# Delta rule and routed experts on one core: groups of 128 tokens, a state update from raw keys, two inverses interleaved

## The chip, the cores and the metric

One core of a Trainium2 chip runs the whole program as one launch. The metric is the device time in microseconds; the median of three runs of the kernel before is 737.12 us (735.65 to 737.18).

## The reference

```python
def _attn_ref(q, k, v, beta):          # q, k, v: (4, 8, 768, 48) f32; beta: (4, 8, 768)
    k_n = k / (np.linalg.norm(k, axis=-1, keepdims=True) + 1e-06)
    state = np.zeros((B, H, D, D)); y = np.zeros_like(q)
    for t in range(S):
        kt, vt, bt = k_n[:, :, t], v[:, :, t], beta[:, :, t, None]
        y[:, :, t] = np.einsum('bhd,bhde->bhe', q[:, :, t], state)
        v_old = np.einsum('bhde,bhd->bhe', state, kt)
        state = state + bt[:, :, :, None] * np.einsum('bhd,bhe->bhde', kt, vt - v_old)
    return y
def _moe_ref(x, token_ids, w1, w2):    # x: (3072, 384); w1: (8, 384, 1024); w2: (8, 1024, 384)
    expert_idx = token_ids * np.int64(2654435761) % np.int64(E)
    for e in range(E):
        mask = expert_idx == e
        out[mask] = np.maximum(x[mask] @ w1[e], 0.0) @ w2[e]
```

The answers of the delta rule, with the heads side by side, are the rows x of the expert stage.

## The kernel before

Phase 1 is the delta rule, phase 2 the experts; between them stands a scratch tensor in DRAM (x_scratch). All arithmetic is float32. Instructions go to each engine's queue in the order in which the program writes them (`tc.manual_schedule()`).

Phase 1 cuts the 768 tokens into 24 chunks of C = 32. On the 128 partitions lie the four batches times 32 tokens of a chunk, for 8 heads (four pairs u, each with two heads r). Four chunks make a group; there are six groups.

For each chunk `load_k` and `load_q` bring K and Q in four transfers each, `turn_k` turns them on TensorE (`psT`, evicted by ScalarE into KQ), and `gram` multiplies keys with keys and queries (`psG`, evicted into Gsb). `masks_of` makes the masked matrix MT from Gsb on GpSimd. This runs AHEAD = 10 chunks before the chain.

For each group `invert` makes, for 32 (chunk, head) pairs at a time, the inverse of a triangular matrix 32 by 32: the head takes the turn NTt, the sums of squares ssq, a Sqrt on ScalarE (root), some ten small VectorE instructions, and Ni and the diagonal of U on GpSimd; then for each of 31 columns j a product into tmp (L244) and a sum into U (L241), the rows cut into an upper and a lower half; the last instruction turns U into TU. The main loop takes the pieces of this generator after each chunk, by a fixed count.

The chain runs over the chunks c. `ask(c, 0)` multiplies the keys with the state (psX); R = V1 - psX on VectorE (L283); `solve` multiplies Tz with R (psW), and ScalarE evicts it as W (L298); `update` adds Kz times W to the state in psS (L309), which stays in PSUM, and four ScalarE copies bring it to SBUF (L318); `ask(c, 1)` and `answer` make psY, evicted as x_sb (L330) and written to x_scratch on SP's queue. Tz, Kz (keys spread over two halves with zeros) and V1 are made on GpSimd a chunk ahead.

`routing()` counts the tokens of each expert and computes the gather lists gidx and gx, with the products gp (L448); the loop takes one of its pieces per chunk from c = 4 on. At c = 16 the rest is taken and the first expert's weights are loaded. Phase 2 gathers 128 rows at a time and runs two matrix products per expert.

Of the kernel before, what the change touches and what calls it, by code (L numbers as in the profile page):

```python
# [18 lines left out]
def kernel(  # L19
# [59 lines left out]

    with ExitStack() as phase1:  # L80
# [7 lines left out]
        AHEAD = 10  # L88
        NK = AHEAD + 3
# [16 lines left out]

        K4s = [st.tile([P, HU, 2, DP], F32, name=f"K4_{i}") for i in range(NK)]
        Q4s = [st.tile([P, HU, 2, DP], F32, name=f"Q4_{i}") for i in range(3)]
        Ss = [st.tile([P, 2, H, 2, D], F32, name=f"S_{i}") for i in range(2)]
        psS = ps_s.tile([P, 2, BANK], F32, name="psS")  # L110
        tid32 = rt.tile([P, NTC, 2], I32)
        beta_i = st.tile([P, NG, C], F32)
        beta_h = rt.tile([C, S], F32)
        beta_t = rt.tile([C, NU, B, H], F32)
        beta_q = rt.tile([P, NG, GC, H], F32)
        iota_i = rt.tile([P, P], I32)
        iota_f = rt.tile([P, P], F32)
# [11 lines left out]
        def load_k(c, eng):  # L129
            dst = K4s[c % NK].rearrange("p u r d -> p (u r) d")  # L130
            for b in range(B):
                eng.dma_start(out=dst[quarter(b), :, 0:D], in_=k_r[b][c * C:(c + 1) * C])

        def load_q(c, eng):
            dst = Q4s[c % 3].rearrange("p u r d -> p (u r) d")
            for b in range(B):
                eng.dma_start(out=dst[quarter(b), :, 0:D], in_=q_r[b][c * C:(c + 1) * C])

        Vs, V1s, Kzs = {}, {}, {}

        def load_v(c):
            Vs[c] = wk.tile([P, H, D], F32, tag="V", bufs=4, name="V")
# [3 lines left out]
        def routing_setup():  # L146
            nc.vector.tensor_copy(iota_f, iota_i)

        KQs, MTs, Gsbs, TUs, Tzs, n_toks = {}, {}, {}, {}, {}, {}

        def turn_k(c, a, src):
            if a == 0:
                KQs[c] = wk.tile([P, HU, 2, P], F32, tag="KQ", bufs=AHEAD + 1, name="KQ")
            ps = ps_z.tile([P, HU, P], F32, tag="z", name="psT")
# [4 lines left out]
        def gram(c):  # L159
            g, cc = divmod(c, GC)  # L160
            if cc == 0:
                Gsbs[g] = wk.tile([P, GC, HU, 2, 2 * C], F32, tag="Gsb", bufs=2, name="Gsb")
            KQ = KQs[c]
            ps = [ps_z.tile([P, HU, 2 * C], F32, tag="z", name=f"psG{r}") for r in range(2)]
            for u in range(HU):
                for r in range(2):
                    for b in range(B):
                        nc.tensor.matmul(  # L168
                            ps[r][quarter(b), u, :], lhsT=KQ[half(r), u, 0, quarter(b)],
                            rhs=KQ[half(r), u, :, quarter(b)], start=(u == 0), stop=True,  # L170
                            skip_group_check=True, tile_position=(DP * r, C * b))
            for r in range(2):
                nc.scalar.activation(Gsbs[g][:, cc, :, r, :], ps[r], ACT.Copy)  # L173

        def masks_of(c):
            G = Gsbs[c // GC][:, c % GC].rearrange("p u r y -> p (u r) y")
            MTs[c] = wk.tile([P, H, 2, C], F32, tag="MT", bufs=AHEAD + 1, name="MT")
            nc.gpsimd.tensor_tensor(MTs[c], G[:, :, None, C:].to_broadcast([P, H, 2, C]),  # L178
                                    mask2[:, None].to_broadcast([P, H, 2, C]), op=ALU.mult)
# [14 lines left out]
        def spread_k(c):  # L194

            Kzs[c] = wk.tile([P, H, 2, D], F32, tag="Kz", bufs=2, name="Kz")
            nc.gpsimd.tensor_tensor(  # L197
                Kzs[c],
                K4s[c % NK].rearrange("p u r d -> p (u r) d")[:, :, None, 0:D].to_broadcast(
                    [P, H, 2, D]),  # L200
                kmask[:, None, :, None].to_broadcast([P, H, 2, D]), op=ALU.mult)

        def invert(g):

            G = Gsbs.pop(g).rearrange("p c u r y -> p (c u r) y")
            NTt = wk.tile([P, C, C], F32, tag="NTt", bufs=1, name="NTt")
            nc.vector.transpose(NTt, G[:, :, 0:C].rearrange("p x j -> p j x"))
            ssq = wk.tile([P, C], F32, tag="ssq", bufs=2, name="ssq")
            nc.vector.tensor_scalar(out=ssq, in0=NTt.rearrange("p j i -> p (j i)")[:, ::C + 1],
                                    scalar1=1e-30, scalar2=None, op0=ALU.max)  # L210
            root = wk.tile([P, C], F32, tag="root", bufs=2, name="root")
            nc.scalar.activation(root, ssq, ACT.Sqrt)
            yield
            rn = wk.tile([P, C], F32, tag="rn", bufs=2, name="rn")
            nc.vector.reciprocal(rn, root)
            nc.vector.tensor_tensor(rn, rn, ssq, op=ALU.mult)
            nc.vector.tensor_tensor(root, root, rn, op=ALU.add)
            nc.vector.tensor_scalar(out=root, in0=root, scalar1=0.5, scalar2=1e-6,
                                    op0=ALU.mult, op1=ALU.add)
            nc.vector.tensor_tensor(rn, root, root, op=ALU.mult)  # L220
            nc.vector.reciprocal(rn, rn)
            d = wk.tile([P, C], F32, tag="d", bufs=2, name="d")
            nc.vector.tensor_tensor(d, rn, beta_i[:, g], op=ALU.mult)
            nd = wk.tile([P, C], F32, tag="nd", bufs=2, name="nd")
            nc.vector.tensor_scalar(out=nd, in0=d, scalar1=-1.0, scalar2=None, op0=ALU.mult)
            Ni = wk.tile([P, C, C], F32, tag="Ni", bufs=1, name="Ni")
            U = wk.tile([P, C, C], F32, tag="U", bufs=1, name="U")
            nc.gpsimd.memset(U, 0.0)
            nc.gpsimd.tensor_tensor(Ni, NTt, nd[:, None, :].to_broadcast([P, C, C]), op=ALU.mult)
            nc.gpsimd.tensor_copy(U.rearrange("p c i -> p (c i)")[:, ::C + 1], d)  # L230
            n_toks[g] = wk.tile([P, NX], F32, tag="ntok", bufs=3, name="ntok")
            nc.vector.transpose(n_toks[g], root)
            yield
            def term(lo, hi, j, last):

                n, m = hi - lo, C - 1 - j
                if not last:
                    tmps[lo] = wk.tile([P, L * L], F32, tag=f"tmp{lo}", bufs=2, name="tmp")
                tmp = tmps[lo][:, 0:n * m].rearrange("p (n m) -> p n m", n=n)
                if last:  # L240
                    nc.vector.tensor_tensor(U[:, lo:hi, j + 1:], U[:, lo:hi, j + 1:], tmp,  # L241
                                            op=ALU.add)
                else:
                    nc.vector.tensor_tensor(tmp, U[:, lo:hi, j:j + 1].to_broadcast([P, n, m]),  # L244
                                            Ni[:, j:j + 1, j + 1:].to_broadcast([P, n, m]),
                                            op=ALU.mult)

            tmps = {}
            lower = iter([(j, last) for j in range(L, C - 1) for last in (False, True)])
            for j in range(C - 1):  # L250
                hi = min(j + 1, L)
                term(0, hi, j, False)
                nxt = next(lower, None)
                if nxt:
                    term(L, nxt[0] + 1, *nxt)
                term(0, hi, j, True)
                yield
            TUs[g] = wk.tile([P, NX, C], F32, tag="TU", bufs=2, name="TU")
            nc.vector.transpose(TUs[g].rearrange("p x i -> p i x"),  # L259
                                U.rearrange("p c i -> p i c"))  # L260
            yield
# [6 lines left out]
        def ask(c, a, ps):  # L268
            S0 = Ss[c % 2]
            for u, b in slots():  # L270
                nc.tensor.matmul(ps[quarter(b), u], lhsT=KQs[c][:, u, a, quarter(b)],
                                 rhs=S0[:, b // 2, 2 * u + b % 2].rearrange("p r d -> p (r d)"),
# [3 lines left out]
        def old_values(c):  # L276
# [5 lines left out]
            R = wk.tile([P, H, D], F32, tag="R", bufs=2, name="R")  # L282
# [5 lines left out]
        def solve(c, R):  # L288
# [8 lines left out]
            W = wk.tile([P, H, D], F32, tag="W", bufs=2, name="W")  # L297
# [3 lines left out]
        def update(c, W):  # L301
            Kz = Kzs.pop(c)
            S1 = Ss[(c + 1) % 2]
            for u in range(HU):
                for e in range(2):
                    for r in range(2):
                        for p in range(2):
                            rows = slice(DP * p, DP * p + DP)
                            nc.tensor.matmul(  # L309
# [174 lines left out]
        with tc.manual_schedule():  # L484
            for t in Q4s + K4s:
                nc.gpsimd.memset(t[:, :, :, D:], 0.0)
            for c in range(3):
                load_q(c, nc.gpsimd)
# [226 lines left out]
```

## Time and profile before

| | us |
|---|---|
| median of 3 runs | 737.12 |
| the profiled execution's own time | 736.42 |
| its span | 734.8 |
| TensorE busy in the span | 564.0 (77%) |
| VectorE busy | 304.5 (41%) |
| GpSimd busy | 232.5 (32%) |
| ScalarE busy | 140.3 (19%) |

The span runs from the first to the last instruction of the profiled execution; the rest of its own time lies around it. Busy time is the time in which an engine works on some instruction, and idle time is only worth something on the engine that others wait for. Shares are means over stages with different limits.

### The profile page before, as it was taken

Reading aid. Unit: us, or ns where it says so; the run is one execution under the profiler, and the core shown is the slowest. Engines: PE = TensorE matmul, PEld = TensorE weight load, DVE = VectorE, ACT = ScalarE, POOL = GpSimd, SP = SyncE. Lnnn points to the kernel's source line nnn. Section 1 sums busy time; section 2 is a strip of 40 time slices with the busy share of each in tenths; the row PEclk is TensorE's granted clock in tenths of the full one; section 3 lists DMA queues with packets and bytes.
Section 4 is the critical chain, followed back from the end, with each engine's and each line's share of the span. In section 5 each row is a group of like instructions: output and inputs, shape, how many; then the busy total and the mean of one; then the engine's idle time right before and its main releaser. Section 6 shows DMA issues by size and latency. Waiting matters only on the chain. (4 is left out here: it accounts for less than half of the span.)

```text
span 734.8 us, 16900 instructions
## 1 busy us (share of the span) xinstructions
PE 564.0 (77%) x7252; PEld 368.1 (50%) x7252; DVE 304.5 (41%) x805; ACT 140.3 (19%) x291; POOL 232.5 (32%) x256
## 2 busy tenths in 40 slices
PE   3660657468456564577729999999999999999996
PEld 2440546457455454566614555546455554645553
DVE  4269695895997677594021101111110111111100
ACT  2430324224224141133400000010000000000000
POOL 7783714445335233343342120303021130101101
PEclk9999968778777576768968999999999999999999
DMA  8621114233232011152159432214333010000000
GB/s 124 121 47 31 35 26 87 47 75 65 46 71 62 17 25 41 26 194 59 41 205 385 155 119 95 75 65 139 97 121 122 12 49 0 32 0 22 14 12 19
DMA packets 87115, 54.72 MB, mean 74 GB/s; under 512 B 69626, under 2 KB 80966, under 8 KB 87040
## 3 DMA queue, kind: packets, MB, share of 16 engines
q1 hardware_dynamic: 81536, 42.02, 21.5%
q0 software_dynamic: 5504, 11.61, 5.3%
q8 instruction: 58, 0.95, 0.6%
q14 instruction: 17, 0.14, 0.1%
HBM read 45.74 MB, written 11.01 MB: 77 GB/s over the span
## 5 line engine op out<-in xcount | busy, mean ns | idle before, releaser
L618 PE MATMUL o_ps<-w_sb,h_sb 128*128 128x384 f32 x512 | 169.9, 486 | 0.0
L607 PE MATMUL h_ps<-xT,w_sb 128*128 128x512 f32 x384 | 167.5, 596 | 0.0
L618 PEld LDWEIGHTS o_ps<-w_sb,h_sb 128*128 128x128 f32 x512 | 95.2, 190 | 61.1 <-issue 1.0
L607 PEld LDWEIGHTS h_ps<-xT,w_sb 128*128 128x128 f32 x384 | 73.5, 192 | 90.7 <-issue 88.8
L244 DVE TENSOR_TENSOR tmp<-U,Ni 128x48 f32<-128x48 f32 (+32 forms) x276 | 98.8, 385 | 42.6 <-POOL U L230 36.9
L591 POOL DMA_INDIRECT xg<-x_scratch,gx x32 | 32.7, 1022 | 168.7 <-PE xT_ps L600 148.8
L294 PE MATMUL psW<-R,Tz 64*64 64x48 f32 x736 | 35.4, 263 | 63.3 <-DVE R L283 63.3
L241 DVE TENSOR_TENSOR U<-U,tmp 128x48 f32<-128x48 f32 (+32 forms) x276 | 83.1, 326 | 0.2
L612 DVE TENSOR_SCALAR h_sb<-h_ps 128x512 f32<-128x512 f32 x32 | 22.1, 692 | 144.8 <-PE h_ps L607 144.8
L622 POOL DMA_INDIRECT out_dram<-o_sb,gidx x32 | 32.1, 1002 | 137.4 <-ACT o_sb L621 87.4
L178 POOL TENSOR_TENSOR MT<-Gsb,mask 128x512 f32<-128x512 f32 x24 | 31.6, 1316 | 127.5 <-ACT Gsb L173 125.8
L294 PEld LDWEIGHTS psW<-R,Tz 64*64 64x64 f32 x736 | 32.3, 178 | 67.9 <-DVE R L283 39.8
L610 ACT ACTIVATE h_sb<-h_ps 128x512 f32<-128x512 f32 x32 | 19.1, 597 | 183.8 <-PE h_ps L607 183.8
L318 ACT ACTIVATE S<-psS 48x384 f32<-48x384 f32 x92 | 44.6, 485 | 26.2 <-PE psS L309 24.6
L601 DVE COPY xT<-xT_ps 128x384 f32<-128x384 f32 x32 | 17.7, 553 | 73.8 <-PE xT_ps L600 72.5
L168 PE MATMUL psG<-KQ 48*32 48x64 f32 x1536 | 26.6, 288 | 24.1 <-ACT KQ L157 23.4
L621 DVE COPY o_sb<-o_ps 128x384 f32<-128x384 f32 x16 | 8.9, 558 | 84.6 <-PE o_ps L618 79.9
L157 ACT ACTIVATE KQ<-psT 128x512 f32<-128x512 f32 x48 | 28.5, 597 | 74.3 <-PE psT L156 74.2
L184 POOL TENSOR_TENSOR Tz<-TU,kmask 128x512 f32<-128x512 f32 x24 | 25.9, 1079 | 52.5 <-DVE TU L259 32.3
L197 POOL TENSOR_TENSOR Kz<-K,kmask 128x768 f32<-128x768 f32 x24 | 36.5, 1519 | 4.0 <-PE psS L309 4.0
L168 PEld LDWEIGHTS psG<-KQ 48*32 48x32 f32 x1536 | 21.2, 137 | 29.5 <-ACT KQ L157 27.4
L309 PE MATMUL psS<-W,Kz 64*48 64x48 f32 x1472 | 29.4, 248 | 7.4 <-ACT W L298 7.3
(123 smaller groups left out, 532.6 us busy)
## 6 DMA issues: line engine op xcount, KB each, us to landing
w_sb<-in_moe_w_dram SPq DMA_DIRECT2D x16, 1536.0 KB, 7.5
K<-in_k_dram SPq DMA_DIRECT2D x96, 48.0 KB, 2.7
V<-in_v_dram SPq DMA_DIRECT2D x96, 48.0 KB, 2.2
x_scratch<-x_sb SPq DMA_DIRECT2D x24, 192.0 KB, 2.6
Q<-in_q_dram SPq DMA_DIRECT2D x52, 48.0 KB, 2.3
Q<-in_q_dram POOLq DMA_DIRECT2D x44, 48.0 KB, 2.6
xg<-x_scratch,gx POOLq DMA_INDIRECT x32, 6.3
out_dram<-o_sb,gidx POOLq DMA_INDIRECT x32, 2.6
```

The lines of the kernel that those rows point to most:

```text
L168: nc.tensor.matmul(ps[r][quarter(b), u, :], lhsT=KQ[half(r), u, 0, quarter(b)], rhs=KQ[half(r), u, :, quarter(b)], start=(u == 0), stop=Tr ...
L178: nc.gpsimd.tensor_tensor(MTs[c], G[:, :, None, C:].to_broadcast([P, H, 2, C]), mask2[:, None].to_broadcast([P, H, 2, C]), op=ALU.mult)
L197: nc.gpsimd.tensor_tensor(Kzs[c], K4s[c % NK].rearrange("p u r d -> p (u r) d")[:, :, None, 0:D].to_broadcast([P, H, 2, D]), kmask[:, None ...
L241: nc.vector.tensor_tensor(U[:, lo:hi, j + 1:], U[:, lo:hi, j + 1:], tmp, op=ALU.add)
L244: nc.vector.tensor_tensor(tmp, U[:, lo:hi, j:j + 1].to_broadcast([P, n, m]), Ni[:, j:j + 1, j + 1:].to_broadcast([P, n, m]), op=ALU.mult)
L294: nc.tensor.matmul(psW[rows, h], lhsT=Tz[rows, h].rearrange("p e i -> p (e i)"), rhs=R[rows, h], start=(h == 0), stop=True, skip_group_che ...
L309: nc.tensor.matmul(psS[half(r), p, D * (2 * u + e):D * (2 * u + e) + D], lhsT=Kz[rows, 2 * u + r, e], rhs=W[rows, 2 * u + r], start=(c == ...
L318: nc.scalar.activation(S1[half(r), :, part, r], new[half(r), :, part], ACT.Copy)
L591: nc.gpsimd.indirect_dma_start(out=xg, out_offset=None, in_=x_dram[:, :], in_offset=bass.IndirectOffsetOnAxis(ap=idx, axis=0), bounds_chec ...
L607: nc.tensor.matmul(h_ps[:, :width], lhsT=w1_sb[:, co, fo * P:(fo + 1) * P], rhs=xT[:, co, :width], start=(co == 0), stop=(co == CO - 1))
L618: nc.tensor.matmul(o_ps, lhsT=h_sb[:, fo, col * P:(col + 1) * P], rhs=w2_sb[:, fo, :], start=(fo == 0), stop=(fo == FO - 1))
L622: scat = nc.gpsimd.indirect_dma_start(out=out[:, :], out_offset=bass.IndirectOffsetOnAxis(ap=idx, axis=0), in_=o_sb, in_offset=None, bound ...
```

## The change

K and Q are loaded for turning by 128 tokens of one batch (`load_turn`, one transfer where there were four) and turned by `turn`; KQ holds a whole group. Raw keys are loaded once more by chunk (`load_k`) as the update's left operand. `gram` evicts keys with keys and keys with queries apart, GK (already in the order that the turn NTt reads) and GQ. `spread_k` and Kz are gone: `update` takes 32 rows of raw keys of a batch for both heads of a pair, 128 columns, and psS has one bank for each batch. `invert` becomes `head`, `strand` and `tail`; `together` deals out one instruction of each strand in turn, and a group's second half runs with the next group's first half. `fill` spends a budget of 5500 by the diff's own cost numbers per chunk, and `fill_until` finishes what the next group needs. The prologue turns four groups and makes the grams of three and the whole of inverse 0 before the chain begins. Routing has four pieces in the prologue and two per chunk from c = 17; gp is cut into 8 parts of 3 products. The first weights are loaded after c = 20. The pools are smaller: z 2, x 1 (in place of 3 and 2), R and W one buffer each. Phase 2 is the same.

```diff
-        def load_k(c, eng):
-            dst = K4s[c % NK].rearrange("p u r d -> p (u r) d")
+        def load_turn(g, a, b, eng):
+            dst = (KTs, QTs)[a][b].rearrange("p u r d -> p (u r) d")
+            eng.dma_start(out=dst[:, :, 0:D], in_=(k_r, q_r)[a][b][g * NB:(g + 1) * NB])
+        def load_k(c):
+            dst = K4s[c % 3].rearrange("p u r d -> p (u r) d")
...
+        def turn(g, a, b, eng=nc.scalar):
+            src = (KTs, QTs)[a][b]
+            ps = ps_z.tile([P, HU, NB], F32, tag="z", name="psT")
             for u in range(HU):
                 nc.tensor.transpose(ps[:, u, :], src[:, u].rearrange("p r d -> p (r d)"), ident)
-            nc.scalar.activation(KQs[c][:, :, a, :], ps, ACT.Copy)
+            copy_out(eng, KQs[g][:, :, a, b, :], ps)
...
             for r in range(2):
-                nc.scalar.activation(Gsbs[g][:, cc, :, r, :], ps[r], ACT.Copy)
+                nc.scalar.activation(GKs[g][:, :, cc, :, r].rearrange("p j u -> p u j"),
+                                     ps[r][:, :, 0], ACT.Copy)
+                nc.scalar.activation(GQs[c][:, :, r], ps[r][:, :, 1], ACT.Copy)
...
+        def head(g, first):
+            nc.vector.transpose(NTt, GKs.pop(g).rearrange("p j c u r -> p j (c u r)"))
+            nc.gpsimd.memset(U, 0.0)
...
             nc.scalar.activation(root, ssq, ACT.Sqrt)
-            yield
+            yield 1600
...
+            (nc.vector if first else nc.gpsimd).tensor_tensor(
+                Ni, NTt, nd[:, None, :].to_broadcast([P, C, C]), op=ALU.mult)
...
+        def strand(g, c0, c1, j0, j1):
+            U, Ni = Us[g], Nis[g]
+            for j in range(max(j0, c0), j1):
+                n, m = min(j + 1, c1) - c0, C - 1 - j
...
+                nc.vector.tensor_tensor(t, U[:, c0:c0 + n, j:j + 1].to_broadcast([P, n, m]),
+                                        Ni[:, j:j + 1, j + 1:].to_broadcast([P, n, m]),
+                                        op=ALU.mult)
+                yield 75 + 1.04 * n * m
+                nc.vector.tensor_tensor(U[:, c0:c0 + n, j + 1:], U[:, c0:c0 + n, j + 1:], t,
+                                        op=ALU.add)
+                yield 75 + 1.04 * n * m
...
+                    yield from head(g, False)
+                both = []
+                if g > 1:
+                    both += [strand(g - 1, 0, L, L, C - 1), strand(g - 1, L, C, L, C - 1)]
+                if g == 1:
+                    both += [strand(g, 0, L // 2, 0, L), strand(g, L // 2, L, L // 2, L)]
+                elif g < NG:
+                    both += [strand(g, 0, L, 0, L)]
+                yield from together(*both)
...
         def update(c, W):
-            Kz = Kzs.pop(c)
...
-                            nc.tensor.matmul(
-                                psS[half(r), p, D * (2 * u + e):D * (2 * u + e) + D],
-                                lhsT=Kz[rows, 2 * u + r, e], rhs=W[rows, 2 * u + r],
-                                start=(c == 0 and u == 0 and e == 0), stop=True,
-                                skip_group_check=True, tile_position=(DP * p, DP * r))
+            S1, K4 = Ss[(c + 1) % 2], K4s[c % 3]
+            for u, b in slots():
+                nc.tensor.matmul(psS[:, b, 2 * D * u:2 * D * u + 2 * D],
+                                 lhsT=K4[quarter(b), u].rearrange("p r d -> p (r d)"),
+                                 rhs=W[quarter(b), 2 * u:2 * u + 2].rearrange("p r d -> p (r d)"),
+                                 start=(c == 0 and u == 0), stop=True, skip_group_check=True,
+                                 tile_position=(C * b, 0))
...
+        GRAM_AT = {0: 12, 1: 13, 2: 14, 3: 15, 5: 16, 6: 17, 7: 18, 8: 19,
+                   10: 20, 11: 21, 12: 22, 13: 23}
+        TURN_AT = {(3, 1): t4[0:2], (4, 0): t4[2:4], (4, 1): t4[4:8],
+                   (7, 1): t5[0:1], (8, 0): t5[1:3], (8, 1): t5[3:5], (9, 0): t5[5:6],
+                   (9, 1): t5[6:8]}
+        LOAD_AT = {0: t4[0:4], 1: t4[4:8], 5: t5[0:4], 6: t5[4:8]}
...
+            for c in range(GC):
+                gram(c)
+            steps(route, 4)
+            fill_until(0)
+            for g in range(1, GC):
...
+                for b in range(B):
+                    for a in range(2):
+                        turn(g, a, b)
+                if g < GC - 1:
+                    for c in range(GC * g, GC * g + GC):
+                        gram(c)
...
+            for c in range(NU):
...
+                W = solve(c, R)
+                for t in TURN_AT.get((c, 0), ()):
+                    turn(*t)
+                if c < NU - 1:
                     update(c, W)
+                answer(c, W, psY)
+                for t in TURN_AT.get((c, 1), ()):
+                    turn(*t)
+                if c in GRAM_AT:
+                    gram(GRAM_AT[c])
+                for t in LOAD_AT.get(c, ()):
+                    load_turn(*t, nc.sync)
+                if c + 1 < NU:
+                    scale_v(c + 1)
+                    if c + 1 == GC * (g + 1):
+                        fill_until(g + 1)
+                    spread_t(c + 1)
+                    masks_of(c + 1)
+                fill(5500)
+                if c >= 17:
+                    steps(route, 2)
```

## Rows read from the trace of the kernel before

**Rows 1.** Busy us of PE, PEld, DVE, ACT, POOL by stage; clock, DMA share, GB/s.

```profile
0.00:77.30 77.30, 33.48 (x724) 24.85 (x724) 43.37 (x130) 19.95 (x43) 49.88 (x87) 1.00 0.45 77
77.30:339.00 261.70, 160.97 (x4628) 141.65 (x4628) 207.63 (x582) 79.04 (x171) 104.71 (x94) 0.73 0.26 59
```

**Rows 2.** The chain that ended last, around the end of phase 1.

```profile
370.98 3.73 DMA x_scratch<-x_sb
```

**Rows 3.** Timeline of ACT, a late step: start, duration, what.

```profile
343.01 0.49 ACT L298 ACTIVATE W<-psW 128x384 f32<-128x384 f32 x1 [2.09 <-PE psW L294]
344.70 2.02 ACT L318 ACTIVATE S<-psS 48x384 f32<-48x384 f32 x4 [1.20 <-PE psS L309]
```

**Rows 4.** Timeline of PE, from 247 to 351 us.

```profile
247.13 2.77 PE L448 MATMUL gp<-hi,lo 128*128 128x52 f32 x12 [11.94 <-DVE lo L443]
...
334.06 1.95 PE L294 MATMUL psW<-R,Tz 64*64 64x48 f32 x32 [2.80 <-DVE R L283]
336.75 1.53 PE L309 MATMUL psS<-W,Kz 64*48 64x48 f32 x64 [0.74 <-ACT W L298]
...
343.65 0.93 PE L309 MATMUL psS<-W,Kz 64*48 64x48 f32 x63 [0.74 <-ACT W L298]
...
347.28 0.87 PE L271 MATMUL psY<-S,KQ 128*32 128x96 f32 x32
348.08 1.13 PE L294 MATMUL psW<-R,Tz 64*64 64x48 f32 x32
349.96 0.96 PE L309 MATMUL psS<-W,Kz 64*48 64x48 f32 x61 [0.74 <-ACT W L298]
```

**Rows 5.** Timeline of DVE, from 71 to 115 us.

```profile
71.12 1.92 DVE L207 STREAM_TRANSPOSE NTt<-Gsb 128x1024 f32<-128x1024 f32 x1
...
74.16 0.35 DVE L215 RECIPROCAL rn<-root 128x32 f32<-128x32 f32 x1 [0.30 <-ACT root L212]
...
81.73 2.38 DVE L244 TENSOR_TENSOR tmp<-U,Ni 128x31 f32<-128x31 f32 x2 [5.38 <-POOL U L230]
...
99.22 0.55 DVE L283 TENSOR_TENSOR R<-V,psX 128x384 f32<-128x384 f32 x1
99.68 0.42 DVE L244 TENSOR_TENSOR tmp<-U,Ni 128x256 f32<-128x256 f32 x1
100.02 0.55 DVE L241 TENSOR_TENSOR U<-U,tmp 128x64 f32<-128x64 f32 x2
100.60 0.54 DVE L244 TENSOR_TENSOR tmp<-U,Ni 128x240 f32<-128x240 f32 x2
...
114.06 2.17 DVE L259 STREAM_TRANSPOSE TU<-U 128x1024 f32<-128x1024 f32 x1
```

**Rows 6.** Busy time of each engine while one inverse runs, columns as before.

```profile
81.73:114.06 32.33, 18.29 (x654) 15.94 (x652) 31.30 (x95) 11.55 (x25) 12.29 (x11) 0.79 0.21 44
```

**Rows 7.** POOL's instructions by line: busy us, mean ns, idle before.

```profile
L197 POOL TENSOR_TENSOR Kz<-K,kmask 128x768 f32<-128x768 f32 x24 | 36.5, 1519 | 4.0 <-PE psS L309 4.0
...
L178 POOL TENSOR_TENSOR MT<-Gsb,mask 128x512 f32<-128x512 f32 x24 | 31.6, 1316 | 127.5 <-ACT Gsb L173 125.8 <-DVE beta_t L521 1.7
L184 POOL TENSOR_TENSOR Tz<-TU,kmask 128x512 f32<-128x512 f32 x24 | 25.9, 1079 | 52.5 <-DVE TU L259 32.3 <-PE psW L294 19.6 <-PE psT L156 0.6
...
L191 POOL TENSOR_TENSOR V<-V,ntok 128x384 f32<-128x384 f32 x24 | 21.4, 892 | 0.0
L229 POOL TENSOR_TENSOR Ni<-NTt,nd 128x1024 f32<-128x1024 f32 x6 | 14.1, 2353 | 5.5 <-DVE nd L225 5.5
```

**Rows 8.** Timeline of the prologue, from 14 to 19 us.

```profile
14.77 1.11 PE L156 MATMUL psT<-ident,K 128*128 128x128 f32 x4
...
15.67 1.06 PE L156 MATMUL psT<-ident,Q 128*128 128x128 f32 x4
...
17.42 1.18 PE L168 MATMUL psG<-KQ 48*32 48x64 f32 x64 [0.69 <-ACT KQ L157]
...
18.57 0.66 ACT L173 ACTIVATE Gsb<-psG 128x256 f32<-128x256 f32 x2 [1.21 <-PE psG L168]
```

More of the change, by code (lines that the diff above doesn't have):

```diff
@@ L155, in turn_k, with copy_out @@
+        def copy_out(eng, out, in_):
+            if eng is nc.scalar:
+                nc.scalar.activation(out, in_, ACT.Copy)
+            else:
+                nc.vector.tensor_copy(out, in_)
+        def turn(g, a, b, eng=nc.scalar):
+            if g not in KQs:
+                KQs[g] = wk.tile([P, HU, 2, B, NB], F32, tag="KQ", bufs=4, name="KQ")
+            src = (KTs, QTs)[a][b]
+            ps = ps_z.tile([P, HU, NB], F32, tag="z", name="psT")
             for u in range(HU):
                 nc.tensor.transpose(ps[:, u, :], src[:, u].rearrange("p r d -> p (r d)"), ident)
-            nc.scalar.activation(KQs[c][:, :, a, :], ps, ACT.Copy)
+            copy_out(eng, KQs[g][:, :, a, b, :], ps)
@@ L192, in scale_v @@
                                     op=ALU.mult)
[L194 to L208, printed above, removed]
+        Us, Nis = {}, {}
@@ L248, in invert @@
[L248 to L257, printed above, removed]
+            Nis[g] = Ni = iv.tile([P, C, C], F32, tag="Ni", bufs=2, name="Ni")
+            (nc.vector if first else nc.gpsimd).tensor_tensor(
+                Ni, NTt, nd[:, None, :].to_broadcast([P, C, C]), op=ALU.mult)
@@ L258, in invert, with together, tail @@
+        def together(*its):
+            its = list(its)
+            while its:
+                for it in list(its):
+                    cost = next(it, None)
+                    if cost is None:
+                        its.remove(it)
+                    else:
+                        yield cost
+        def tail(g):
+            Nis.pop(g)
             TUs[g] = wk.tile([P, NX, C], F32, tag="TU", bufs=2, name="TU")
             nc.vector.transpose(TUs[g].rearrange("p x i -> p i x"),
-                                U.rearrange("p c i -> p i c"))
@@ L261, in invert, with inverses @@
-            yield
+                                Us.pop(g).rearrange("p c i -> p i c"))
+        made = set()
+        def inverses():
+            for g in range(NG + 1):
+                if g == 0:
+                    yield from head(0, True)
+                    yield from together(strand(0, 0, L, 0, C - 1), strand(0, L, C, L, C - 1))
+                    tail(0)
+                    made.add(0)
+                    yield 2000
+                    continue
+                if g < NG:
+                    while GC * g + GC - 1 not in GQs:
+                        yield -1
+                    yield from head(g, False)
[7 more added lines that the diff above has]
+                yield from together(*both)
+                if g > 1:
+                    tail(g - 1)
+                    made.add(g - 1)
+                    yield 2000
@@ L476, in routing, with fill, fill_until, steps @@
             yield
-        def take(it, n):
+        fills = inverses()
+        left = [0.0]
+        def fill(budget):
+            left[0] += budget
+            while left[0] > 0:
+                cost = next(fills, None)
+                if cost is None or cost < 0:
+                    left[0] = 0.0
+                    return
+                left[0] -= cost
+        def fill_until(g):
+            while g not in made:
+                assert next(fills) >= 0
+            left[0] = min(left[0], 0.0)
+        def steps(it, n):
             for _ in range(n):
@@ L518 @@
                                     kmask[:, :, None].to_broadcast([P, 2, C]), op=ALU.mult)
-            for t in Ss:
-                nc.gpsimd.memset(t, 0.0)
+            for b in range(B):
+                turn(0, 0, b)
+            for b in range(B):
+                turn(0, 1, b, nc.vector)
             nc.vector.transpose(beta_t.rearrange("i n b h -> i n (b h)"),
@@ L528 @@
             route = routing()
-            inv = iter(())
-            for c in range(-AHEAD, NU):
-                a = c + AHEAD
-                chain = c >= 0
-                if a + 2 < NU and chain:
-                    load_k(a + 2, nc.sync)
-                if 3 <= a + 1 < NU:
-                    load_q(a + 1, nc.sync if chain else nc.gpsimd)
-                if chain and c + 3 < NU:
-                    load_v(c + 3)
-                if chain:
-                    R = old_values(c)
-                    psY = ps_y.tile([P, HU, 2 * D], F32, tag="y", name="psY")
-                    if c > 0:
-                        ask(c, 1, psY)
-                if a < NU:
-                    turn_k(a, 0, K4s[a % NK])
-                if chain:
-                    W = solve(c, R)
-                if a < NU:
-                    turn_k(a, 1, Q4s[a % 3])
-                if chain and c < NU - 1:
-                    update(c, W)
-                if a < NU:
-                    gram(a)
-                if chain:
-                    answer(c, W, psY)
-                if 0 <= c + 1 < NU:
-                    spread_t(c + 1)
-                    spread_k(c + 1)
-                    scale_v(c + 1)
-                if a < NU:
-                    masks_of(a)
-                k = (c + 6) % GC
-                if k == 0:
-                    take(inv, 40)
-                    g = (c + 6) // GC
-                    if 0 <= g < NG:
-                        inv = invert(g)
-                        take(inv, 1)
-                else:
-                    take(inv, {1: 6, 2: 10, 3: 10}[k])
-                if c >= 4:
-                    take(route, 1)
-                if c == 16:
-                    take(route, 1000)
-                    rt_stack.close()
```

216 lines of the change are left out of this document (114 added, 102 removed).

## The prediction

> **What bounds the kernel now.** I read the stages first [rows 1]. Up to 77.3 us, when the first solve (L294) reaches TensorE, no engine is full: VectorE 43 us, GpSimd 50, DMA at 0.45 of its time. From there to 339.0, the end of the last inverse, VectorE is busy 208 of 262 us, TensorE 161 at a mean granted clock of 0.73. The expert stage begins when the last answer has landed in x_scratch, 370.98 + 3.73 = 374.71 [rows 2]; nothing in the change touches what follows, so its 360.1 us to the end of the span (734.8) stay, and so do the 1.6 us around it (this execution's own time is 736.42, 0.7 under the median of 737.12).
>
> Then I looked for what a step of the chain (one 32-token chunk) costs once VectorE is free. Two updates in a row start at 343.65 and 349.96: 6.31 us, at the quicker of the two paces that TensorE's rows show. At the slower one a solve takes 1.95 for 1.13 and an update 1.53 for 0.96 [rows 4]; with the asks in proportion I take 8.0 for such a step. From the first R at 99.22 [rows 5] to the landing there are 275 us for 23 steps, 12 each. So the chain is not the bound: R stands in VectorE's queue behind pieces of the inverse, and the solve waits for it.
>
> What makes an inverse long? One whole inverse without routing runs from 81.73 to the turn at 114.06 [rows 5]: 32.33 us. Its 92 products and sums hold 2 x 5456 elements (counted from `term`). A 256-element product is followed 0.34 us later by a sum that doesn't need it; the sums of 64 and 256, then the product that needs the last of them, take 0.58 [rows 5]. I read 0.075 us + 1.04 ns per element for an instruction, and 0.10 more when it needs the one just ahead, once in each of 31 columns: 18.25 + 3.1 = 21.35. With two R's (0.46 each) 22.3 are explained. The other 10.0 fall beside GpSimd's 12.3 busy us of that window [rows 6]: some 0.8 us of VectorE lost for each us of GpSimd arithmetic. At 81.73 two products of 31 and 15 elements take 2.38. Before that VectorE idled 5.38 for U's diagonal [rows 5], behind the mask products, whose wait for the same step's gram comes to 125.8 us [rows 7].
>
> **The change part by part.** *Kz goes*: of 4.81 us of GpSimd a step, 1.52 [rows 7]; 3.29 stay and cost VectorE 0.8 x 3.29 = 2.6 a step instead of 3.8. *Masks*: MT is made a step ahead from GQ, so GpSimd no longer sits behind a gram; Ni and the diagonal then cost 2.35 + 0.24, about 2.3 after what overlaps [rows 7]. Group 0's Ni goes to VectorE: 0.075 + 1.07 = 1.1.
>
> *Interleaving.* Two or three independent strands alternate, so the 0.10 has another instruction to hide behind: I take 18.25 per inverse. The bounds are 18.25 and 21.35. Inverse 0 gains nothing: its upper strand is alone for half its columns. The Trainium skill speaks against this part: VectorE: DVE Perf Modes, section "The DRAIN you can't avoid", says that after each instruction the pipe is flushed and that chaining can't avoid it. The 0.34 behind an instruction that alone takes 0.42, and the two sums in 0.55 [rows 5], don't agree with it.
>
> *Update.* 32 products of 48 columns (64 records, 0.96 us) become 16 of 96 columns (32 records), with 32 rows and 128 weight columns each. No row has this shape. The ask also has 32 records of 96 columns on four tiles and takes 0.87 [rows 4]; the other end is 128x128 weights one after another, 2.77 us for 12 records [rows 4], 7.4 for 32. I take no change; the shape is nearest the ask's. The state copies stay four of 0.5 [rows 3].
>
> *Smaller pools.* psX and psW share one buffer, R and W too: each is read out before the next is written in the chain's own order, so 0; if not, the price is the wait for one eviction, 0.5 [rows 3]. Two z buffers instead of three serialize grams: 1.18 on TensorE, then four evictions of 128 elements; two of 256 take 0.66 [rows 8], so I take 0.3 each, 2.45 a gram. A turn stays 0.9 from start to start [rows 8].
>
> *Prologue.* Group 0 is eight loads of 196.6 KB. DMA moved 77 GB/s at share 0.45 [rows 1], 171 at full share: 9 us at best and 20 at the mean rate; near the first, since nothing else loads then, I take 12. Landed by 15, turned by 17. Issue on SP is hidden behind the transfers. Four grams, 9.8: 27. Four pieces of routing (3), the turn of GK (1.92 [rows 5]) and ssq put Sqrt(0) at 32 on ScalarE, and the evictions of group 1's turns are queued behind it. Then turns, grams, turns, grams, turns: 7.2 + 9.8 + 7.2 + 9.8 + 7.2 = 41. The first solve stands behind all that in TensorE's queue: P = 74 (77.3 now). Inverse 0 is done near 60 and waits. If turns and grams run at the quick pace P is 65; as many us later if the loads keep the mean rate.
>
> *The wait that is added.* Each head now sits at the start of a step's fill, and its Sqrt is queued on ScalarE behind that step's W, state copies, answer and gram evictions. From the solve's start to the first state copy are 2.9 us quick, 4.3 slow [rows 3, 4]; then copies 2.0, the answer's eviction 0.5 like W's, the gram's 1.2, Sqrt 0.4 by estimate: 7.0 or 8.4, plus 0.6 from R. VectorE gets there after 2.5 and stops; behind it stand the rest of the fill and the next R, for which the next solve waits. After it come the rest of the head, 2.2 (74.16 to 76.35 [rows 5]), and Ni, 2.3. This hits steps 0, 2, 8 and 13, where a head starts with VectorE on time, and not 3, where it comes late.
>
> *The sum.* The diff's own budget (5.5 us of its cost numbers a step, more where a group falls due) puts the strands, in us, at: step 0 2.5, 1 5.6, 2 2.5, 3 19.8, 4 5.5, 5 5.8, 6 4.6, 7 none, 8 2.6, 9 5.6, 10 5.5, 11 4.6, 12 none, 13 2.6, 14 5.6, 15 15.5, 16 4.5. A step costs 0.46 + 2.6 + its strands, 2.1 for a turn of U [rows 5], 1.9 for a turn of GK. R(1) = P + 8.4 + 2.2 + 2.6 + 2.5 = P + 15.7. Then step 1 8.6; 2 13.5 (Sqrt); 3 31.8 (two thirds of inverse 1, half of 2, head 3); 4 10.5 (six turns in the chain, two ahead of the update and four ahead of the next ask); 5 8.8; 6 9.7; 7 7.5; 8 17 (Sqrt, four turns); 9 9; 10 8.6; 11 9.7; 12 7; 13 14.8 (Sqrt); 14 8.7; 15 20.6; 16 9.7; 17 and 18 6.5 each, the bare chain; 19 to 22 7.2 each, since six products of gp, 1.4 slow per three [rows 4], stand ahead of the next ask with some 1 us to spare. That is 237, so R(23) = P + 253. R, solve, W, answer, eviction and landing: 8.2. Phase 1 ends at 74 + 261 = 335 instead of 374.7: 39.5 less. Most of routing (hi, lo, gp, slots), which now stands ahead of R's in the crowded steps, has moved to steps 17 to 22, where VectorE is free. 734.8 - 39.5 + 1.6 = 697.
>
> *Hidden.* Loads for groups 4 and 5 go on SP in steps 0, 1, 5, 6, behind x_sb's write and ahead of K and V two steps on; uncovered, 196.6 KB at 171 GB/s is 1.2 us. The first expert's weights (3.1 MB, 18 us at that rate) are issued after step 20, not 16, about 28 us before phase 1 ends.
>
> **The rivals.** *B, quicker*: the Sqrt finds ScalarE free and the prologue is quick. Steps 0, 2, 8, 13 lose 7, 3, 5, 3, P another 9: 670. For it: ScalarE is busy 79 of 262 us [rows 1]; against: in-order queues. *C, interleaving gives nothing*: the 0.10 is charged in any order. 91 us of strands in the loop become 106: 712. The two sums above speak against; it is what the skill's rule on the DRAIN would do here, too. *D, slower*: the update's weights load one after another. At the rate of gp's records [rows 4] it takes 7.4 for 1.53; the slow step goes from 8.0 to 13.9, 17 plain steps then cost 236 and the whole comes to about 810. It decides from 3.9 us an update on: 2.4 more, of which 0.6 hides in VectorE's steps, over 22 steps is the 40 gained. For it: no row with 128 columns on a 32-row tile. Against: each batch writes its own bank and four row tiles are in turn, as in the ask. The Trainium skill's TensorEngine Tiling (Array Packing), section "Key Properties", lets different tiles load and multiply in parallel, but has every change of tiling mode drain the engine; no row here shows either for this shape. *E*: turns, grams or loads in the prologue come 10 to 30 us later than summed, 705 to 727.
>
> **How the numbers follow.** The forecast 0.50 (own range 680 to 710), B 0.20, C 0.11, E 0.09, D 0.10. The point is the forecast's sum. The range takes in B with 0.4 a step less lost beside GpSimd over 20 steps (662) and E's upper end (727); D and a B beyond that stay out. A measurement of this kernel tells a change from none at about 0.2%, 1.5 us. Faster are the forecast, B, C and E, less 0.01 for an E that ends within that: 0.89; same 0.01; slower is D, 0.10.
>
> **What would show it.** First solve near 74 and R(1) near 90; VectorE idle for ScalarE's root at the start of steps 0, 2, 8 and 13, 2 to 15 us each; strands without the 0.10; one step of some 32 us at step 3 and one of 20 at 15; bare steps of 6.3 to 7.2 from 17 on; update near 0.9 quick. It is wrong if the update's records take over 0.1 us, if the first solve comes after 90, or if VectorE still loses more than 3 us a step beside GpSimd.

## The result, and the profile after

The changed kernel took 705.57 us (median of 4 runs, 702.91 to 708.42); the kernel before took 736.38 on the same chips. The ratio is 0.9586, 95% interval 0.9541 to 0.9631: faster. The forecast was 697.0, 8.6 under it, and 705.57 lies in the forecast's own range. The profiled execution took 702.91, with a span of 701.2 where the sum gave 695.3.

The stages after (columns as in [rows 1]): up to the first solve, to R(17), to the landing of the last answer, and the expert stage.

```profile
0.00:67.70 67.70, 46.98 (x900) 34.20 (x900) 43.76 (x151) 27.64 (x77) 13.51 (x25) 0.85 0.86 114
67.70:286.40 218.70, 128.28 (x3534) 112.26 (x3536) 157.03 (x550) 70.09 (x173) 85.14 (x65) 0.74 0.32 60
286.40:338.03 51.63, 40.10 (x1104) 35.55 (x1093) 21.07 (x56) 18.48 (x38) 18.55 (x16) 0.93 0.51 133
338.03:701.20 363.17, 344.86 (x992) 180.95 (x992) 50.72 (x88) 26.75 (x48) 64.99 (x64) 0.97 0.26 87
```

Phase 1 ends at 338.0 (forecast 335, before 374.7 [rows 2]). In the crowded stage VectorE is busy 157 of 219 us: it was 208 of 262 [rows 1], so it now idles there, 62 us, a little more than before. These rows of VectorE's timeline show where the longest waits are (the bracket holds the idle time and who ended it):

```profile
74.24 0.35 DVE L221 RECIPROCAL rn<-root 128x32 f32<-128x32 f32 x1 [14.40 <-ACT root L218]
...
78.95 1.76 DVE L255 TENSOR_TENSOR tmp<-U,Ni 128x31 f32<-128x31 f32 x2 [2.52 <-POOL U L244]
...
100.73 0.35 DVE L221 RECIPROCAL rn<-root 128x32 f32<-128x32 f32 x1 [3.01 <-ACT root L218]
...
175.19 0.55 DVE L327 TENSOR_TENSOR R<-V,psX 128x384 f32<-128x384 f32 x1 [9.71 <-PE psX L315]
...
185.61 1.25 DVE L211 STREAM_TRANSPOSE NTt<-GK 128x1024 f32<-128x1024 f32 x1 [9.86 <-ACT GK L183]
...
187.37 0.35 DVE L221 RECIPROCAL rn<-root 128x32 f32<-128x32 f32 x1 [0.30 <-ACT root L218]
...
235.59 1.25 DVE L211 STREAM_TRANSPOSE NTt<-GK 128x1024 f32<-128x1024 f32 x1 [6.81 <-ACT GK L183]
```

The first and third are the Sqrt wait of steps 0 and 2; 7.9 of the 14.40 lie ahead of the first solve. The fourth, at the end of step 7, is a wait of another kind: R waits for psX, and so the chain, with the turns and grams in it, sets the pace there. R waits so in steps 4, 7, 9, 10, 12 and 14, 1.2 to 9.7 each, 28 us in all, nearly half of the 62. At steps 8 and 13 VectorE waits at the same place in the step, but one instruction earlier: NTt needs GK of grams 19 and 23, and these are made in steps 8 and 13 themselves, behind four turns at step 8. Sqrt then finds ScalarE free (0.30).

The steps (step c runs from R(c) to R(c+1) on VectorE, worked out from the starts of L327, in other kernels of its counterpart, one profiled execution each), in us; the last three columns are experiments told below:

| step | forecast | after | Sqrt early | Ni on VectorE | waits filled |
|---|---|---|---|---|---|
| first solve | 74 | 67.7 | 69.4 | 67.5 | 66.4 |
| 0, from that to R(1) | 15.7 | 16.2 | 5.7 | 5.8 | 5.8 |
| 1 | 8.6 | 9.6 | 7.6 | 7.0 | 7.0 |
| 2 | 13.5 | 13.2 | 14.6 | 11.1 | 11.1 |
| 3 | 31.8 | 31.2 | 28.2 | 27.9 | 28.2 |
| 4 to 6 | 29.0 | 27.1 | 28.4 | 28.4 | 29.2 |
| 7 | 7.5 | 10.2 | 8.9 | 9.2 | 10.8 |
| 8 | 17 | 21.7 | 13.5 | 13.0 | 11.9 |
| 9 to 11 | 27.3 | 24.2 | 28.3 | 28.9 | 29.7 |
| 12 | 7 | 7.1 | 8.3 | 8.1 | 7.3 |
| 13 | 14.8 | 18.6 | 13.3 | 11.1 | 13.8 |
| 14 | 8.7 | 8.8 | 8.6 | 8.8 | 9.7 |
| 15 | 20.6 | 22.0 | 20.7 | 21.8 | 8.5 |
| 16 | 9.7 | 8.8 | 8.8 | 8.8 | 8.3 |
| 17 to 22 | 41.8 | 42.9 | 42.5 | 43.0 | 44.0 |

The update, in TensorE's timeline at the slow and at the quick pace (before: 1.53 and 0.96 [rows 4]):

```profile
87.23 2.04 PE L348 MATMUL psS<-W,K 32*128 32x96 f32 x32 [0.64 <-ACT W L342]
...
295.75 1.15 PE L348 MATMUL psS<-W,K 32*128 32x96 f32 x32 [0.64 <-ACT W L342]
```

### The profile page after: what moved, and what is told of

Its sections match the earlier page's. It is cut to its first block, busy times and chain, and to the rows that moved or that the text cites. A ratio compares the mean times of both kernels' runs of the same rounds, so it can differ in the third digit from the quotient of the medians.

```text
span 701.2 us, 15467 instructions
## 1 busy us (share of the span) xinstructions
PE 560.2 (80%) x6516; PEld 363.0 (52%) x6516; DVE 272.6 (39%) x845; ACT 143.0 (20%) x335; POOL 182.2 (26%) x170
## 4 chain that ended last, share of the span: by engine, by line
issue 43%; POOL 7%; DMA 0%; POOLq 0%; DVE 0%; DVEq 0%
POOL out_dram L700 4%; POOL xg L669 2%; DMA x_scratch<-x_sb 0%; DVE xg L732 0%; POOLq L700 0%; POOLq L788 0%; POOLq L669 0%; DVEq L709 0%
## 5 line engine op out<-in xcount | busy, mean ns | idle before, releaser
L338 PE MATMUL psW<-R,Tz 64*64 64x48 f32 x736 | 32.1, 245 | 77.6 <-DVE R L327 35.0
L255 DVE TENSOR_TENSOR tmp<-U,Ni 128x39 f32<-128x39 f32 (+29 forms) x284 | 81.0, 328 | 4.2 <-POOL U L244 3.3
L259 DVE TENSOR_TENSOR U<-U,tmp 128x39 f32<-128x39 f32 (+29 forms) x284 | 79.6, 324 | 0.9
L196 POOL TENSOR_TENSOR Tz<-TU,kmask 128x512 f32<-128x512 f32 x24 | 33.4, 1390 | 74.6 <-DVE TU L276 71.5
L203 POOL TENSOR_TENSOR V<-V,ntok 128x384 f32<-128x384 f32 x24 | 28.5, 1187 | 82.7 <-DMA V<-in_v_dram 47.6
L348 PE MATMUL psS<-W,K 32*128 32x96 f32 x736 | 32.0, 321 | 12.8 <-ACT W L342 12.8
L178 PE MATMUL psG<-KQ 48*32 48x64 f32 x1536 | 30.2, 264 | 13.1 <-issue 5.3
L699 ACT COPY o_sb<-o_ps 128x384 f32<-128x384 f32 x16 | 7.6, 478 | 142.4 <-PE o_ps L696 142.4
L342 ACT ACTIVATE W<-psW 128x384 f32<-128x384 f32 x24 | 11.8, 490 | 121.9 <-PE psW L338 121.9
L348 PEld LDWEIGHTS psS<-W,K 32*128 32x128 f32 x736 | 27.8, 223 | 16.3 <-ACT W L342 15.8
```

The source lines that it names most:

```text
L178: nc.tensor.matmul(ps[r][quarter(b), u], lhsT=KQ[half(r), u, 0, b, tk], rhs=KQ[half(r), u, :, b, tk], start=(u == 0), stop=True, skip_grou ...
L196: nc.gpsimd.tensor_tensor(Tzs[c], TUs[c // GC][:, x0:x0 + H, None, :].to_broadcast([P, H, 2, C]), kmask[:, None, :, None].to_broadcast([P, ...
L203: nc.gpsimd.tensor_tensor(V1s[c], Vs.pop(c), n[:, :, None].to_broadcast([P, H, D]), op=ALU.mult)
L255: nc.vector.tensor_tensor(t, U[:, c0:c0 + n, j:j + 1].to_broadcast([P, n, m]), Ni[:, j:j + 1, j + 1:].to_broadcast([P, n, m]), op=ALU.mult)
L259: nc.vector.tensor_tensor(U[:, c0:c0 + n, j + 1:], U[:, c0:c0 + n, j + 1:], t, op=ALU.add)
L338: nc.tensor.matmul(psW[rows, h], lhsT=Tz[rows, h].rearrange("p e i -> p (e i)"), rhs=R[rows, h], start=(h == 0), stop=True, skip_group_che ...
```

## The experiments

Ratios are to the kernel before, which ran beside each.

**Grams one step earlier.**

```diff
+        HEAD_AT = {4: 8, 5: 13}
...
-        GRAM_AT = {..., 5: 16, 6: 17, 7: 18, 8: 19, 10: 20, 11: 21, 12: 22, 13: 23}
+        GRAM_AT = {..., 5: (16, 17), 6: (18,), 7: (19,), 10: (20, 21), 11: (22,), 12: (23,)}
```

> The grams that complete groups 4 and 5 are made one step before their heads (chunk 17 joins 16 in step 5, 21 joins 20 in step 10, so 19 and 23 come in steps 7 and 12); the heads stay in the fills of steps 8 and 13. Theory (turn of GK waits for the step's own gram, and with that gone the Sqrt wait that was forecast stands in its place): steps 8 and 13 cost about 17 and 15 instead of 21.7 and 18.6, the doubled grams cost about 1 each in steps 5 and 10, the whole about 700 us. Rival 1 (the turn's wait hides nothing, since Sqrt is free by then): steps 8 and 13 fall to 13 and 11, about 690. Rival 2 (TensorE's six turns and slow pace set these steps): no change, 704 to 708.

703.86 us, ratio 0.9531 (0.9496 to 0.9567): not to be told from the changed kernel (0.9541 to 0.9631). Steps 8 and 13 took 17.9 and 16.5, near the theory's 17 and 15, and VectorE's timeline shows the forecast's Sqrt wait in the place of the turn's:

```profile
185.78 0.35 DVE L221 RECIPROCAL rn<-root 128x32 f32<-128x32 f32 x1 [6.51 <-ACT root L218]
...
239.28 0.35 DVE L221 RECIPROCAL rn<-root 128x32 f32<-128x32 f32 x1 [5.06 <-ACT root L218]
```

The profiled execution (707.15) gave the 5.9 gained back: steps 5 and 10, with a gram more each, took 3.0 and 2.7 more, not 1, step 12 2.0 and step 22 3.0. Steps 12 and 22 hold no gram more; TensorE's mean granted clock was 0.71 and 0.65 there, where it was 1.00 in the changed kernel's execution, so these 5 us are not shown to come of the edit. At steps 8 and 13 two waits stood one behind the other, and taking the first away lays the second bare.

**Sqrt early as well.** Each head's first piece (head_a: turn of GK, U's memset, ssq, Sqrt) goes to the top of a step; group 1's goes ahead of group 3's turns in the prologue.

```diff
+        HEAD_AT = {2: 2, 4: 8, 5: 13}
...
+                for x in HEAD_AT:
+                    if HEAD_AT[x] == c:
+                        head_a(x)
                 W = solve(c, R)
```

> Grams as in the kernel with the early grams, and besides each head's first piece (turn of GK, ssq, Sqrt) is issued at the top of steps 2, 8, 13, ahead of W on ScalarE, and for group 1 before the last group's turns in the prologue. Theory (Sqrt's place in ScalarE's queue costs these steps their length): R(1) comes some 9 us earlier, step 2 costs 9 to 10 instead of 13.2, step 8 some 12 instead of 21.7, step 13 some 11 instead of 18.6; whole 675 to 686. Rival (the wait only moves on, to Ni on GpSimd, or to TensorE with the turns): 695 or more, with Ni or psX in the place of root as releaser.

681.11 us, ratio 0.9243 (0.9221 to 0.9265): 24.5 less than the changed kernel and 22.8 less than with the early grams alone. Step 0 lost 10.5, step 8 8.1, step 13 5.3. Step 2 gained nothing (14.6): there the rival is right, as VectorE's, then GpSimd's timeline show.

```profile
93.71 0.19 DVE L264 TENSOR_TENSOR tmp<-U,Ni 128x31 f32<-128x31 f32 x1 [6.22 <-POOL U L253]
```

```profile
88.11 0.83 POOL L203 TENSOR_TENSOR V<-V,ntok 128x384 f32<-128x384 f32 x1 [11.98 <-DMA V<-in_v_dram]
88.90 1.04 POOL L196 TENSOR_TENSOR Tz<-TU,kmask 128x512 f32<-128x512 f32 x1
89.90 1.27 POOL L190 TENSOR_TENSOR MT<-GQ,mask 128x512 f32<-128x512 f32 x1
91.12 2.37 POOL L251 TENSOR_TENSOR Ni<-NTt,nd 128x1024 f32<-128x1024 f32 x1
```

Ni could have begun at 87.0, when its operand nd was there, but it is queued behind V's product, which waits for a load; the wait went from ScalarE's queue to GpSimd's.

**Ni on VectorE** in every head, on top of that.

```diff
-            (nc.vector if first else nc.gpsimd).tensor_tensor(
+            nc.vector.tensor_tensor(
                 Ni, NTt, nd[:, None, :].to_broadcast([P, C, C]), op=ALU.mult)
```

> The kernel with the early Sqrt, and Ni and U's diagonal made on VectorE in every head instead of on GpSimd. Theory (at steps 2, 8 and 13 the wait for U's diagonal, 6.2 and 3.7 at the first two, has taken Sqrt's place, since Ni is queued on GpSimd behind V's load, Tz and MT): these steps cost 9, 11 and 11 instead of 14.6, 13.6 and 13.3, less 1.2 of new work on VectorE each; whole 668 to 674. Rival (psX or the rest of the strands ends these steps): 677 or more.

671.12 us, ratio 0.9084 (0.9022 to 0.9147): as the theory had it for the whole, with steps 2 and 8 2 longer than it said. In step 2 VectorE is now busy 10.7 of 11.1 us: its own work fills the step.

**The waiting steps filled**, on top of that: while the fill waits for the next group's gram it goes on with the lower strands of the group before.

```diff
                     while HEAD_AT.get(g, -1) > now[0] or GC * g + GC - 1 not in GQs:
-                        yield -1
+                        yield next(low, -1)
```

> The kernel with Ni on VectorE, and besides the lower strands of a group run in the steps in which the fill waited for the next group's gram (7 and 12), and V(23) is loaded ahead of the first expert's weights. Theory (VectorE idles some 8 us in each of steps 7 and 12 while step 15 holds 20 us of strands): steps 8 to 11 and 13 to 15 lose 8 to 11 together, step 22 1.2: 657 to 664. Rival (the strands only lengthen steps 7 and 12 by what they shorten the others): 667 or more.

662.24 us, ratio 0.8973 (0.8922 to 0.9024). The windows of step 7, with Ni on VectorE and with the wait filled (us, then busy time of PE, PEld, DVE, ACT, POOL):

```profile
147.71:156.90 9.19, 6.88 (x244) 5.83 (x240) 2.77 (x4) 4.86 (x15) 3.98 (x4) 1.00 0.76 147
```

```profile
147.74:158.59 10.85, 7.42 (x260) 6.15 (x252) 10.81 (x34) 4.89 (x15) 4.18 (x4) 1.00 0.69 132
```

VectorE works through a step in which it had idled 6.4 of 9.2; step 7 grows by 1.7 and step 15 falls from 21.8 to 8.5. V(23) ahead of the weights brought 0.3, not 1.2: R(23) then waits for the ask.

**Group 3's turns behind the first solve**, on top of that.

```diff
-        TURN_AT = {(3, 1): ...}
+        TURN_AT = {(0, 1): t3[0:4], (1, 0): t3[4:6], (1, 1): t3[6:8], (3, 1): ...}
```

> The kernel with the filled waits, and group 3's eight turns moved from ahead of the first solve to steps 0 (four, behind the answer) and 1 (two ahead of the update, two behind the answer), with grams 12 to 15 in steps 1 to 3 and group 4's loads a step later. Theory (these turns alone hold the first solve from 60 to 66, while Tz(0) is there at 59; VectorE then waits 4.1 for psX in step 0): first solve near 60, R(1) near 67, and 4 to 6 less in the whole, 656 to 659. Rival (R(4) is set by VectorE's strands, which start no earlier, and by the turns in step 1): 661 to 664.

660.50 us, ratio 0.8991 (0.8967 to 0.9015): not to be told from the one before it. The first solve came at 60.6 as expected, but R(1) at 70.9 instead of 72.2 and R(4) at 117.7 instead of 118.6: the turns stand ahead of ask(1) instead, and R(1), R(2) and R(3) wait for psX 0.56, 0.99 and 0.50 alone, so VectorE's own queue (with 1.5 for Sqrt's result in step 0) sets these steps. That is the rival's account, and the time lies half a us under the rival's range.

**Strands one by one**, in the changed kernel.

```diff
-            while its:
-                for it in list(its):
-                    cost = next(it, None)
...
+            for it in its:
+                yield from it
```

> The strands of a fill run one after another instead of taking turns; the instructions are the same. Theory (0.10 us more for an instruction that needs the one just ahead): 92 instructions an inverse pay it, 9 us an inverse, some 35 to 46 us over five inverses in the loop: 740 to 751. Rival (VectorE charges the same in any order, as the skill's rule on the DRAIN has it): 703 to 708, and spacings within a step unchanged.

745.96 us, ratio 1.0113 (1.0086 to 1.0141): 40.4 more than the changed kernel. (This is more than the change undone: the kernel before had lower terms between the upper's product and sum already.) VectorE's timeline, one by one and then in turns:

```profile
114.71 0.29 DVE L255 TENSOR_TENSOR tmp<-U,Ni 128x128 f32<-128x128 f32 x1
115.04 0.29 DVE L259 TENSOR_TENSOR U<-U,tmp 128x128 f32<-128x128 f32 x1
```

```profile
114.18 0.68 DVE L255 TENSOR_TENSOR tmp<-U,Ni 128x128 f32<-128x128 f32 x3
114.78 0.68 DVE L259 TENSOR_TENSOR U<-U,tmp 128x128 f32<-128x128 f32 x3
```

A 128-element sum that needs the product just ahead follows it by 0.33, 0.12 more than 0.075 + 1.04 x 0.128. In turns, three instructions of 128, 64 and 192 elements (counted from the strands) take 0.60, from one row's start to the next; the same formula gives 0.62. The Trainium skill, VectorE: DVE Perf Modes, section "The DRAIN you can't avoid", says that chaining operations without semaphores doesn't skip the flush behind each. No run here tests semaphores; the rows and the 40.4 us show that the order counts all the same, so rival C's reading of that section, one charge in any order, doesn't hold here.

**Kz back**, in the changed kernel, into a tile that nothing reads.

```diff
                     spread_t(c + 1)
+                    spread_k(c + 1)
                     masks_of(c + 1)
```

> The product of K with kmask (128x768 on GpSimd, 1.52 us before the change) is put back into every step, into a tile that nothing reads. Theory of the prediction (VectorE loses 0.8 us for each us of GpSimd): 1.2 us a step over some 19 steps in which VectorE sets the pace, 725 to 730. Rival (beside dense strands GpSimd is the one that waits, as its operations of 4 us there suggest, and VectorE loses a third or less): 706 to 713.

716.52 us, ratio 0.9732 (0.9698 to 0.9767): 11.0 more. By line, GpSimd's part (count, busy us, mean ns) is

```profile
L202 POOL TENSOR_TENSOR Kz<-K,kmask 128x768 f32<-128x768 f32 x23 | 34.9, 1516 | 0.0
```

11.0 / 34.9 = 0.31 us for each of GpSimd: as a mean that is nearer the rival than the 0.8 of the forecast. Step by step it is not one price (worked out from the two traces, in us):

| step | VectorE idle in it, changed kernel | Kz in it | longer by |
|---|---|---|---|
| 1 | 0.7 | 1.6 | 0.6 |
| 3 | 0.8 | 3.1 | 2.7 |
| 6 | 0.1 | 1.5 | 1.2 |
| 15 | 0.1 | 3.2 | 2.6 |
| 16 | 0.2 | 1.5 | 2.0 |
| the other 18 together | | 21.1 | 3.1 |

Where VectorE hardly idled, 10.8 us of Kz made the steps 9.1 longer, 0.84 for each, and VectorE's busy time grew by 9.7 with no instruction more. So beside dense strands it is VectorE that pays, at the forecast's price, and not GpSimd, as the rival had it. Where VectorE idled, most of Kz cost nothing.

**The update alone**, in the kernel before (with psS in four banks, so two z buffers and one x).

```diff
-                                lhsT=Kz[rows, 2 * u + r, e], rhs=W[rows, 2 * u + r],
+                                 lhsT=K4[quarter(b), u].rearrange("p r d -> p (r d)"),
+                                 rhs=W[quarter(b), 2 * u:2 * u + 2].rearrange("p r d -> p (r d)"),
...
-                    spread_k(c + 1)
```

> The kernel before with one part of the change alone: the state is updated from raw keys (no Kz, 32 records of 96 columns, psS in four banks, so two z buffers and one x). Theory of the prediction (0.8 us of VectorE for each of GpSimd): 1.2 a step over some 19 steps, 711 to 716. By the price that the return of Kz to the changed kernel showed (11 us): 723 to 728. Rival (the update's longer records, or the fewer buffers, take it all back): 734 or more.

720.31 us, ratio 0.9762 (0.9706 to 0.9818): 16.6 less, between the two theories; 16.6 for 36.5 us of GpSimd [rows 7] is 0.45, the net of the whole edit. In the six steps in which VectorE idled less than 0.6 in both kernels and Kz took over 1 us (2, 5, 8, 9, 16 and 17), 11.9 us of Kz less made 9.9 less, 0.83 for each, while steps 1, 4, 18 and 19 took 4.5 more: R waits for psX in three of them, and the mean granted clock was lower in step 1 (0.50 for 0.68) and step 4 (0.55 for 0.78). The last three steps took 6.44 where they took 6.31 to 6.37 before: that is what the longer update costs the bare chain at the quick pace.

**Routing back** to steps 4 to 16, one piece a step, in the changed kernel.

```diff
-                if c >= 17:
-                    steps(route, 2)
+                if c >= 4:
+                    steps(route, 1)
```

> Routing goes back to one piece a step in steps 4 to 16 (two a step from 17 on in the changed kernel). Theory (its 17 us of VectorE outside the waits lie ahead of R's in crowded steps again, and steps 17 to 22 lose their six products of gp): steps 4 to 16 together 10 to 15 longer, steps 17 to 22 0.6 each shorter, 709 to 717. Rival (VectorE idles enough in steps 7, 8, 12, 13 to hide it): 700 to 706.

722.74 us, ratio 0.9806 (0.975 to 0.9861): 17.2 more, beyond the theory's range. Steps 4 to 16 together took 16.7 more, not 10 to 15. Only steps 19 to 21 gave 0.6 to 0.7 each back; 17, 18 and 22 took 1.9, 0.5 and 1.2 more. In steps 9 to 12 and 14, which took 11.0 of the 16.7, VectorE waits 1.3 to 6.7 for the products gp (L487) ahead of R: not VectorE's own work alone, but its waiting for TensorE inside routing holds R up.

## Why the prediction was right, point by point

- **The bound.** That VectorE's queue and not the chain sets the pace held for the steps with dense strands or a head. It did not hold in steps 4, 7, 9, 10, 12 and 14 of the changed kernel, where R waits for psX, 28 us in all; the forecast had seen this for 4, 7 and 12 alone. Early Sqrt, Ni and the filled waits took waits from VectorE and paid; an earlier first solve (the turns moved) did not.
- **Interleaving.** The mechanism is right: 0.12 where an instruction needs the one ahead, none in turns. One by one all 92 of an inverse pay; before, 31 did. A third of 40.4 is 13.6 by this estimate, where the forecast took five times 3.1, 15.5. Rival C falls.
- **Kz.** The 0.8 us for each of GpSimd, worked out by calling all that one window didn't explain contention [rows 5, 6], came out right where VectorE hardly idles: 0.84 and 0.83. What was wrong is where it is paid: the forecast charged 2.6 in nearly every step, and over the whole kernel Kz cost 0.31 and brought 0.45 for each us, since the chain or a wait sets the other steps.
- **The update.** Taken as unchanged; it takes 1.15 for 0.96 and 2.04 for 1.53. The ask's row was the right neighbour, the weights' one by one were not: rival D, which needed 3.9, falls.
- **The wait that is added.** Steps 0 and 2 took what the forecast gave them (16.2 for 15.7, 13.2 for 13.5), step 0 by parts that offset each other: Sqrt's result was read 6.5 behind the first solve, not 8.4, and the rest took 9.7, not 7.3. At steps 8 and 13 this part failed: the forecast put them at 17 and 14.8 for Sqrt alone and missed that the turn of GK has to wait for the group's last gram, made in the same step; they took 21.7 and 18.6, 8.5 more. The early grams took 5.9 of that back and showed the Sqrt wait behind it; no run took the other 2.6 apart.
- **Routing** was moved "where VectorE is free" without a price of its own. Back in the crowded steps it cost 17.
- **Prologue.** 67.7 for 74. The first turn began at 4.5, group 0 was turned at 14.3 instead of 17, and its Sqrt ran at 29.5 instead of 32. From there to the first solve it took 38.2 instead of 42, with turns 0.65 to 0.9 apart. Rival E falls.
- **Rival B** had Sqrt find ScalarE free; the kernel with the early Sqrt shows what that is worth together with the earlier grams: 24.5.
- **The rest of the 5.9** between 695.3 and 701.2: the first solve -6.3, step 0 +0.5, steps 1 to 22 +8.0 (steps 8 and 13 +8.5, step 7 +2.7 with a gram at the slow pace, steps 5, 10 and 11 6.5 less: GpSimd ran 2.1, 2.3 and 0.0 us in them, where 3.3 had been charged), the last step with its landing +0.6, the expert stage 363.1 for 360.1. Of these 3.0, 0.9 lie ahead of the stage's first matmul and 1.9 behind the issue of its last write; why is open. That the sum came so near is in part luck: the early first solve and the three short steps, 12.8, offset most of the 14.2 that steps 7, 8, 13 and the expert stage took more.
- **Not tested alone:** the masks made a step ahead, the prologue's order and the smaller pools. How the 31 us divide is shown only for routing and Kz, each undone, and by estimate for interleaving.

The change gained 31 us. The three repairs, Sqrt with the grams (24.5), Ni (10.0) and the idle steps (8.9, V(23)'s earlier load included), brought 43 more without another way of computing anything: the waits and idle stretches in the new order of heads, grams and Ni held back more than the change as a whole had gained. The kernel with the waits filled is 10% under the kernel before, and at 662.24 against 705.57 6% under the changed one.

## What to carry to other kernels

When a change moves a short operation to another engine's in-order queue, write down what is queued ahead of it in that very step; the wait is not that operation's 0.2 us but the whole queue's. When one wait is removed, look for the next behind the same consumer before counting the gain: here it was gram, then Sqrt, then Ni. A price per us beside another engine is paid only in the steps in which the engine that pays sets the pace: count those steps first. An idle stretch of the engine that sets the pace is worth more than a cheaper instruction on it: moving strands into steps 7 and 12 brought 8.9 us with no instruction less.

## What the runs showed of the hardware that was not expected

VectorE and GpSimd hold each other up, both ways. In the changed kernel two strand products that took 0.45 in the kernel with the early Sqrt took 2.59 beside Ni (VectorE's, then GpSimd's timeline):

```profile
102.84 2.59 DVE L255 TENSOR_TENSOR tmp<-U,Ni 128x240 f32<-128x240 f32 x2
```

```profile
102.89 2.52 POOL L242 TENSOR_TENSOR Ni<-NTt,nd 128x1024 f32<-128x1024 f32 x1 [9.42 <-DVE nd L238]
...
140.59 4.70 POOL L196 TENSOR_TENSOR Tz<-TU,kmask 128x512 f32<-128x512 f32 x1 [0.89 <-PE psW L338]
```

The last row is the reverse: Tz, 1.04 in the median of 24, lasted 4.70, to 145.29, while VectorE ran strands without a pause at its plain rate until 144.39. The Trainium skill, SBUF — State Buffer, section "SBUF: two separate sides", has a lock that whichever starts first holds for its whole instruction. The rows agree; and they show that a dense row of VectorE instructions can keep GpSimd out through many of them. That is the rarer case: two of the 24 Tz took over 4 us, no Kz in the kernel with Kz back took over 1.8, and it was VectorE that grew longer beside them. So it does not explain why a us of Kz cost 0.31 in the mean; the steps in which VectorE idles do.
